# Splitting the first Q weights over two DMA queues, and normalising the first 256 columns first

## The chip, the cores and the metric

The kernel runs on one core of one Trainium2 chip. The metric is the device time of one execution in microseconds (us), the median of three runs; lower is better. TensorE (PE in the profile) multiplies matrices, VectorE (DVE) and ScalarE (ACT) work on elements, GpSimd (POOL) does small side work, and SyncE (SP) mostly issues DMA transfers. ACT can issue DMA transfers too, on a queue of its own; in the kernel before it issues none.

## The reference

Two layers, each an attention block and a feed-forward block on x of 2048 rows by 1024 columns in bf16, with the same weights in both layers:

```python
x = x + A(layernorm(x), wqkv, wo)      # 32 heads of 32; a row attends to itself and to the rows
                                       # 2, 4, ... 14 before it (8 positions, softmax)
x = x + B(layernorm(x), w1, b1, w2, b2)  # 1024 -> 3584, gelu, -> 1024
x = x + A(layernorm(x), wqkv, wo)
x = x + B(layernorm(x), w1, b1, w2, b2)
```

where `layernorm(x) = (x - mean) / sqrt(var + 1e-5)` along the 1024 columns, and `A` begins with `qkv = layernorm(x) @ wqkv`.

## The kernel before

The 2048 rows are cut into 16 tiles of 128 rows (`x[0]` to `x[15]`) and 4 groups of 512 rows. Everything the change touches lies at the very start, in the first group: x tiles 0 to 3 must be loaded, normalised and transposed (a matrix product needs the 1024 columns along the partitions, as 8 slices k = 0 to 7 of 128), and the Q weights, also 8 slices k, must be loaded. To begin early, the first pass over Q takes only tiles 0 and 1 (256 rows), two slices k at a time.

The loads, all issued by SP; one Q weight transfer carries two slices (512 KB), an x tile is 256 KB:

```python
def load_wq_piece(wt, k):
    sp.dma_start(wt[:, k % (KD // 2):k % (KD // 2) + 2, :], wqkv_v[:, k:k + 2, 0:D])

load_x(0, 0, 2)                                   # x[0], x[1]
wq_first = [wpool.tile([P, KD // 2, D], BF16, name="wt") for _ in range(2)]
for k in range(0, KD, 2):                         # k = 0,1 | x[2] | 2,3 | x[3] | 4,5 | 6,7
    load_wq_piece(wq_first[k // (KD // 2)], k)
    if k < 4:
        load_x(0, 2 + k // 2, 3 + k // 2)
```

`vec`, `act`, `pool` and `sp` are wrappers that keep the instructions of an engine in program order while `on` is set. The helper that records them is line 92, so nearly all work in the profile is on L92; matrix products are on L117, and transposes on TensorE on L211. The normalisation of the first group:

```python
def ln_first():
    vec.on = act.on = True
    def stats(tt):                # DVE: mean and variance; ACT: square root
        ... vec.bn_stats(...) x2; vec.bn_aggr(...)
        act.activation(stds[tt][:], mvs[tt][:, 1:2], ACT.Sqrt, bias=eps_t[:])
    def norm(tt, bounds=(0, D)):  # DVE: 1/std, then (x - mean) * rstd over each column range
        ...
    stats(0)
    stats(1)
    xn0 = norm(0)
    xn1 = norm(1, (0, 2 * P, D))
    transpose_on_pe(xn0, xa[0][:, 0, :, :], [(0, 2, act.copy), (2, 8, act.copy)])
    transpose_on_pe(xn1, xa[0][:, 1, :, :], [(0, 2, vec.tensor_copy)])
    transpose_on_pe(xn1, xa[0][:, 1, :, :], [(2, 8, act.copy)])
    stats(2)
    stats(3)
    for tt in range(2, 4):
        first_late.append((norm(tt), xa[0][:, tt, :, :]))
    vec.on = act.on = False
    act.hold()
```

`transpose_on_pe` writes slices of a normalised tile, transposed, into PSUM, and copies them into `xnT`. The first pass over Q, on tiles 0 and 1, with the transposes of tiles 2 and 3 put in between (`first_late`):

```python
for kq in range(4 if n == 0 else 0):      # two slices k each
    for c in range(7):                    # seven of the eight 128-column chunks of Q
        first[c] = qkv_chunk(wq, c, xnT, first.get(c), kq * (KD // 4), (kq + 1) * (KD // 4), 0, 2)
        if (kq, c) == (2, 3):
            transpose_on_pe(*first_late.pop(0), [(0, KD, act.copy)])
        if (kq, c) == (3, 4):
            ...
            transpose_on_pe(*first_late.pop(0), [(0, KD, act.copy)])
```

The launch, in order: 14 matrix products on zeros keep TensorE busy until the first data come (`warm_up(14)`), then `ln_first()`, then small constants on GpSimd (`build_constants()`), then the rest of the kernel, which the change doesn't touch.

```python
pool.on = True
warm_up(14)
ln_first()
first = build_constants()
... load_x(1); the stages of the four groups and the two layers
```

Transfers that SP or ACT issue signal their landing on one of eight semaphores, which the building layer deals out in turn over both engines. A transfer that is given a semaphore again is held back by a wait, at its issuing engine, until the transfer that had that semaphore before has landed.

Of the kernel before, what the change touches and what calls it, by code (L numbers as in the profile page):

```python
# [8 lines left out]
ACT = mybir.ActivationFunctionType  # L9
ALU = mybir.AluOpType  # L10
AX = mybir.AxisListType
BF16 = mybir.dt.bfloat16
F32 = mybir.dt.float32
# [4 lines left out]
def kernel(  # L18
# [18 lines left out]
    P = 128  # L37
# [68 lines left out]
    def dep_order(dependent, dependency, why):  # L106
        tc.add_manual_dep(dependent.ins, dependency.ins.name,
                          mybir.DependencyInfo(mybir.DependencyClass.NoSync, mybir.DependencyReason.SCHED_ONLY), reason=why)
# [12 lines left out]
    def load_x(g, t0=0, t1=NTT):  # L121
        for tt in range(t0, t1):
            t = g * NTT + tt
            sp.dma_start(x[t][:], x_in[t * P:(t + 1) * P, :])
# [6 lines left out]
            tiles.append(wt)  # L131
        return tiles

    def load_wq_piece(wt, k):
        sp.dma_start(wt[:, k % (KD // 2):k % (KD // 2) + 2, :], wqkv_v[:, k:k + 2, 0:D])

    load_x(0, 0, 2)
    wq_first = [wpool.tile([P, KD // 2, D], BF16, name="wt") for _ in range(2)]
    for k in range(0, KD, 2):
        load_wq_piece(wq_first[k // (KD // 2)], k)  # L140
        if k < 4:
            load_x(0, 2 + k // 2, 3 + k // 2)

    warm = bigp.tile([P, P], BF16, name="big")
    vec.memset(warm[:], 0.0)
    mhalf = const.tile([P, 1], F32, name="mhalf")
# [1 line left out]
    eps_t = const.tile([P, 1], F32, name="eps_t")  # L148
    pool.memset(eps_t[:], EPS)
    one = const.tile([P, 1], F32, name="one")  # L150
    act.activation(one[:], eps_t[:], ACT.Sqrt)
    ident = const.tile([P, P], BF16, name="ident")
    make_identity(nc, ident[:])
# [4 lines left out]
    mv_ahead = const.tile([P, NTT, 2], F32, name="mv_ahead")  # L158
    rstd_ahead = const.tile([P, NTT, 1], F32, name="rstd_ahead")

    def build_constants():
        pool.memset(mask[:], 0.0)
        first = smp.tile([H, W - 1, HALO], F32, name="z")
        pool.memset(first[:], 0.0)
        for w in range(W - 1):
            pool.memset(first[:, w, 0:HALO - DIL * w], -1e9)
        return first

    def load_b1(q):
        js = slice(q * (KF // 4), (q + 1) * (KF // 4))  # L170
# [37 lines left out]
    def transpose_on_pe(xn, out, parts):  # L208
        pst = psum.tile([P, KD, P], BF16, name="acc", bufs=8)
        for k in range(parts[0][0], parts[-1][1]):  # L210
            pe(nc.tensor.transpose(pst[:, k, :], xn[:, k * P:(k + 1) * P], ident[:]))  # L211
        for k0, k1, copy in parts:
            copy(out[:, k0:k1, :], pst[:, k0:k1, :])
# [5 lines left out]
        xn = ln_norm(t, mv, rstd)  # L219
        last_transpose[0] = sp.dma_start_transpose(xnT[:, tt, :, :], xn[:].rearrange("s (k p) -> s k p", p=P))  # L220

    first_late = []

    def ln_first():

        xa[0] = new_xnT()
        vec.on = act.on = True
        mvs = {}
        stds = {}

        def stats(tt):
            st6 = lnp.tile([P, 2, 6], F32, name="stats")
            for h in range(2):
                vec.bn_stats(st6[:, h, :], x[tt][:, h * HALF:(h + 1) * HALF])
            mvs[tt] = lnp.tile([P, 2], F32, name="mv")
            vec.bn_aggr(mvs[tt][:], st6[:])
            stds[tt] = lnp.tile([P, 1], F32, name="std")
            act.activation(stds[tt][:], mvs[tt][:, 1:2], ACT.Sqrt, bias=eps_t[:])

        def norm(tt, bounds=(0, D)):  # L240
            rstd = lnp.tile([P, 1], F32, name="rstd")
            vec.reciprocal(rstd[:], stds[tt][:])
            xn = lnp.tile([P, D], BF16, name="xn", bufs=3)
            for lo, hi in zip(bounds[:-1], bounds[1:]):
                vec.tensor_scalar(out=xn[:, lo:hi], in0=x[tt][:, lo:hi], scalar1=mvs[tt][:, 0:1], scalar2=rstd[:],
                                  op0=ALU.subtract, op1=ALU.mult)
            return xn

        stats(0)
        stats(1)  # L250
        xn0 = norm(0)
        xn1 = norm(1, (0, 2 * P, D))
        transpose_on_pe(xn0, xa[0][:, 0, :, :], [(0, 2, act.copy), (2, 8, act.copy)])
        transpose_on_pe(xn1, xa[0][:, 1, :, :], [(0, 2, vec.tensor_copy)])
        transpose_on_pe(xn1, xa[0][:, 1, :, :], [(2, 8, act.copy)])
        stats(2)
        stats(3)
        for tt in range(2, 4):
            first_late.append((norm(tt), xa[0][:, tt, :, :]))
        vec.on = act.on = False  # L260
        act.hold()

    def new_xnT(pool=None):
        return (pool or xnp).tile([P, NTT, KD, P], BF16, name="xnT")
# [35 lines left out]
    def gen_qkv(n, defer=False, qk_pool=None, v_late=False, qk_next=None, v_first=False, mix=0):  # L300
        g = n % NG
        xnT = xa.pop(n)
        s = st[n]
        s["prods"] = []
        qk_pool = qk_pool or attp
        if v_first:
            wv = load_qkv(2)
        wq = wq_first if n == 0 else load_qkv(0)
        if not v_first:
            wk = load_qkv(1)  # L310

        def values():
            vT = attp.tile([P, NCH, HALO + T], BF16, name="vT", bufs=2)
            s["vT"] = vT
            act.on = n > 2
            if g == 0:
                pool.memset(vT[:, :, 0:HALO], 0.0)
            else:
                (act.copy if n > 1 else pool.tensor_copy)(vT[:, :, 0:HALO], st[n - 1]["vT"][:, :, T:T + HALO])
            act.on = False  # L320
            for c in range(NCH):
                ps = qkv_chunk(wv, c, xnT)
                act.copy(vT[:, c, HALO:], ps[:])
                yield

        if v_first:
            yield from values()
            wk = load_qkv(1)
        if n == 0:
            load_x(2)  # L330
            early_tiles = ln_early((1, None), (2, qk_next))
            for _ in range(NTT):
                next(early_tiles)
            wv = load_qkv(2)
            for _ in early_tiles:
                pass
            load_x(3)
        qT = qk_pool.tile([P, NCH, T], BF16, name="qT")
        first = {}
        for kq in range(4 if n == 0 else 0):  # L340
            for c in range(7):
                first[c] = qkv_chunk(wq, c, xnT, first.get(c), kq * (KD // 4), (kq + 1) * (KD // 4), 0, 2)
                if (kq, c) == (2, 3):
                    transpose_on_pe(*first_late.pop(0), [(0, KD, act.copy)])
                if (kq, c) == (3, 4):
                    for done in range(2):
                        act.copy(qT[:, done, 0:2 * P], first[done][:, 0:2 * P])
                    transpose_on_pe(*first_late.pop(0), [(0, KD, act.copy)])
                    act.hold()
        if n == 0:  # L350
            first[7] = qkv_chunk(wq, 7, xnT, t0=0, t1=2)
        for c in list(first)[2:]:
            act.copy(qT[:, c, 0:2 * P], first[c][:, 0:2 * P])
        kT = qk_pool.tile([P, NCH, HALO + T], BF16, name="kT")
        s["qT"], s["kT"] = qT, kT
        act.on = n > 2
        if g == 0:
            pool.memset(kT[:, :, 0:HALO], 0.0)
        else:
            (act.copy if n > 1 else pool.tensor_copy)(kT[:, :, 0:HALO], st[n - 1]["kT"][:, :, T:T + HALO] if n < 3 else khalo[:])  # L360
        act.on = False

        def query(c):
            t0 = 2 if n == 0 else 0
            ps = qkv_chunk(wq, c, xnT, t0=t0)
            act.copy(qT[:, c, t0 * P:], ps[:, t0 * P:])

        def key(c):
            ps = qkv_chunk(wk, c, xnT)
            act.copy(kT[:, c, HALO:], ps[:])  # L370
            if not defer:
                new_prod(n, c)

        ahead = mix or NCH
        turns = [(query, c) for c in range(ahead)]
        for c in range(NCH):
            turns.append((key, c))
            if ahead + c < NCH:
                turns.append((query, ahead + c))
        for i, (chunk, c) in enumerate(turns):  # L380
            if i == NCH and n > 0 and not v_late and not v_first:
                wv = load_qkv(2)
            chunk(c)
            yield
        if g + 1 < NG and n > 1:
            act.copy(khalo[:], kT[:, :, T:T + HALO])
        if not v_first:
            if v_late:
                wv = load_qkv(2)
            yield from values()  # L390
# [160 lines left out]
    def warm_up(count):  # L551
        ps = acc_tile()
        for _ in range(count):
            mm(ps[:], lhsT=warm[:], rhs=warm[:].unsqueeze(1).to_broadcast([P, NTT, P]), start=True, stop=True)
# [59 lines left out]

    pool.on = True
    warm_up(14)
    ln_first()
    first = build_constants()
    with tc.tile_pool(name="early", bufs=1) as early:
        load_x(1)  # L620
        stage(gen_qkv(0, qk_next=early), sides=at(9, ln_stats_ahead, 2, NTT - 2) + at(14, pool.dma_start, mask[0::NTT, :, :], first[:]) + at(11, ln_end) + at(14, load_b2))
# [60 lines left out]
```

## Time and profile before

| | |
|---|---|
| time, median of 3 runs | 1230.46 us (1230.24 to 1230.65) |
| span of the profiled execution | 1228.4 us |
| TensorE busy | 1221.6 us, 99% |
| DVE / ACT / GpSimd busy | 861.5 / 315.6 / 120.9 us |
| first real matrix product on the weights begins at | 8.26 us |
| DMA moved | 226.64 MB, mean 185 GB/s |

The page gives each engine's busy time, then the span in 40 slices, the DMA queues, and the chain of work that ended last, followed back from the last instruction. A slice is 30.7 us long, so the whole start that the change touches lies inside the first one; it is read from the timeline (start, duration, engine, line, operation, `out<-in`, count, and in brackets how long the engine had been idle and what released it) and from a table of busy times, granted clock and DMA rate in stretches of half a microsecond. The duration of a merged entry runs from the start of its first instruction to the end of its last. A DMA issue has two times: how long the issuing engine needed to issue it, and how long after that start its data had landed.

### The profile page before, as it was taken

The page shows a single profiled execution, that of the slowest core. Times are in us where ns is not written, and L with a number is a line of the kernel's source. Part 1 is how long each engine was busy: PE and PEld are TensorE (multiplying, and loading weights), DVE is VectorE, ACT ScalarE, POOL GpSimd, SP SyncE. Part 2 cuts the span into 40 slices and gives each one's busy share as a digit, 9 for nine tenths or more (in the row PEclk, how much of TensorE's full clock was granted, in tenths as well). Part 3 has the DMA queues.
Part 4 walks back from the last instruction along what each step waited for, and adds up shares of the span by engine and source line. Part 5 has one row for each costly group of instructions (what it writes and reads, how often), then busy time and mean ns, then how long its engine had stood idle before and what let it go on. Part 6 is the DMA issues. An engine that isn't in the chain of part 4 may idle for free.

```text
span 1228.4 us, 13955 instructions
## 1 busy us (share of the span) xinstructions
PE 1221.6 (99%) x5720; PEld 632.7 (52%) x5770; DVE 861.5 (70%) x912; ACT 315.6 (26%) x497; POOL 120.9 (10%) x219
## 2 busy tenths in 40 slices
PE   9999999999999999999999999999999999999998
PEld 7666544456444564446544465444654444444444
DVE  7999896998898999375993759937599797011001
ACT  5343253014310233202431024410244001300310
POOL 2330025010101101100001000000000002000000
PEclk9999999999999999999999999999999999999999
DMA  9965674766638645856557565576664558446441
GB/s 302 290 206 164 176 233 151 202 178 199 219 128 245 188 150 166 239 170 175 161 158 230 172 171 181 157 216 201 171 200 147 186 194 209 149 159 194 156 135 52
DMA packets 223647, 226.64 MB, mean 185 GB/s; under 512 B 71824, under 2 KB 190752, under 8 KB 221536
## 3 DMA queue, kind: packets, MB, share of 16 engines
q1 hardware_dynamic: 214704, 208.69, 56.3%
q0 software_dynamic: 8880, 17.07, 4.2%
q8 instruction: 45, 0.74, 0.2%
q14 instruction: 18, 0.15, 0.0%
HBM read 189.01 MB, written 4.19 MB: 157 GB/s over the span
## 4 chain that ended last, share of the span: by engine, by line
PE 99%; DVE 0%; issue 0%; DMA 0%
PE acc L117 99%; DMA x<-in_A_x_dram 0%; DVE stats L92 0%; PE acc L211 0%; DVE xn L92 0%; DVE x L92 0%; DVE mv L92 0%; DVE rstd L92 0%
## 5 line engine op out<-in xcount | busy, mean ns | idle before, releaser
L117 PE MATMUL acc<-xnT,wt 128*128 128x512 bf16 (+1 forms) x3392 | 720.3, 375 | 0.1
L117 PEld LDWEIGHTS <-wt 128*128 128x128 bf16 x3392 | 400.8, 120 | 317.4
L117 PE MATMUL acc<-wt,hT 128*128 128x512 bf16 (+1 forms) x1780 | 386.0, 376 | 2.1
L117 PEld LDWEIGHTS <-hT 128*128 128x128 bf16 x1820 | 178.1, 98 | 209.0
L92 DVE TENSOR_TENSOR big<-big 128x1024 bf16<-128x1024 bf16 (+2 forms) x184 | 244.8, 1359 | 2.2
L92 ACT ACTIVATE hT<-acc,b1T 128x512 bf16<-128x512 f32 x224 | 152.1, 687 | 325.9 <-PE acc L117 325.8
L92 DVE TENSOR_TENSOR big<-qT,kT 128x4096 bf16<-128x4096 bf16 x64 | 143.8, 2283 | 36.3 <-ACT kT L92 35.9
L92 DVE TENSOR_TENSOR big<-abc,vT 128x4096 bf16<-128x4096 bf16 x64 | 144.6, 2284 | 11.0 <-DMA abc<-a 7.1
L92 DVE TENSOR_TENSOR tmp<-acc,b2bc 128x512 f32<-128x512 f32 x56 | 38.6, 689 | 159.8 <-PE acc L117 156.7
L92 ACT CAST qT<-acc 128x512 bf16<-128x512 f32 (+1 forms) x72 | 38.0, 543 | 276.8 <-PE acc L117 274.6
L117 PE MATMUL acc<-wt,oT 128*128 128x512 bf16 x440 | 97.6, 379 | 0.4
L92 DVE BATCH_NORM_STATS2 stats<-x 128x6 f32<-128x512 bf16 x116 | 77.4, 681 | 6.0 <-DMA x<-in_A_x_dram 5.0
L117 PEld LDWEIGHTS <-oT 128*128 128x128 bf16 x448 | 43.8, 98 | 53.0 <-issue 0.3
L92 DVE TENSOR_TENSOR x<-acc,big 128x512 bf16<-128x512 f32 (+1 forms) x9 | 5.7, 632 | 90.0 <-PE acc L117 90.0
L92 POOL TENSOR_TENSOR rstd<-mv,eps_t 128x1 f32<-128x1 f32 x54 | 16.7, 308 | 524.2 <-DVE mv L92 524.2
L92 ACT CAST vT<-acc 128x512 bf16<-128x512 f32 x64 | 37.4, 585 | 101.9 <-PE acc L117 101.9
L92 ACT CAST kT<-acc 128x512 bf16<-128x512 f32 x64 | 37.3, 584 | 64.5 <-PE acc L117 64.5
L92 DVE TENSOR_TENSOR x<-acc,x 128x512 bf16<-128x512 f32 x64 | 42.9, 670 | 5.1 <-PE acc L117 4.7
L92 DVE TENSOR_SCALAR xn<-x,mv,rstd 128x1024 bf16<-128x1024 bf16 (+2 forms) x53 | 28.5, 540 | 20.1 <-POOL rstd L92 19.9
L92 DVE TENSOR_TENSOR x<-tmp,x 128x512 bf16<-128x512 f32 x56 | 38.6, 689 | 1.4
L92 POOL DMA_DIRECT2D big<-big x24 | 13.3, 563 | 212.5 <-DVE big L92 212.5
L92 ACT ACT_TABLE_LOAD x17 | 21.8, 1283 | 38.9 <-DVE e L92 30.5
(62 smaller groups left out, 285.4 us busy)
## 6 DMA issues: line engine op xcount, KB each, us to landing
wt<-in_B_w_dram SPq DMA_DIRECT2D x56, 1024.0 KB, 5.6
wt<-in_B_w_dram SPq DMA_DIRECT2D x64, 896.0 KB, 4.8
wt<-in_A_wqkv_dram SPq DMA_DIRECT2D x46, 1024.0 KB, 5.6
wt<-in_A_wo_dram SPq DMA_DIRECT2D x16, 1024.0 KB, 5.0
abc<-a POOLq DMA_DIRECT2D x32, 256.0 KB, 4.6
big<-big POOLq DMA_DIRECT2D x24, 256.0 KB, 3.8
x<-in_A_x_dram SPq DMA_DIRECT2D x16, 256.0 KB, 7.1
out_dram<-x SPq DMA_DIRECT2D x31, 128.0 KB, 1.8
```

Source lines behind the costliest of these rows:

```text
L92: inst = f(*args, **kwargs)
L117: return pe(nc.tensor.matmul(*args, **kwargs))
```

## The change

The change means to let the first real matrix products start earlier, with less of x and less of the weights. It has these parts:

- The first x tile comes in two transfers of 512 columns, so that its statistics can begin with the first half.
- Each Q weight slice is a transfer of its own (256 KB). The even ones and the last are issued by SP, slices 1, 3 and 5 by ACT, which waits for GpSimd's last small fill first ("behind the first x tiles").
- Columns 0 to 255 of both tiles are normalised first. Before the first matrix product on weights stand 10 transposes (slices 0, 1 of both tiles, then 2 to 7 of tile 0) in place of 16; the other six of tile 1 stand behind the fourth chunk of the first pass.
- The small constants are built ahead of `ln_first()`.

```diff
-    def load_wq_piece(wt, k):
-        sp.dma_start(wt[:, k % (KD // 2):k % (KD // 2) + 2, :], wqkv_v[:, k:k + 2, 0:D])
-
-    load_x(0, 0, 2)
+    def load_wq_piece(k, engine):
+        return engine.dma_start(wq_first[k // (KD // 2)][:, k % (KD // 2), :], wqkv_v[:, k, 0:D])
+
+    for h in range(2):
+        sp.dma_start(x[0][:, h * HALF:(h + 1) * HALF], x_in[0:P, h * HALF:(h + 1) * HALF])
+    load_x(0, 1, 2)
     wq_first = [wpool.tile([P, KD // 2, D], BF16, name="wt") for _ in range(2)]
     for k in range(0, KD, 2):
-        load_wq_piece(wq_first[k // (KD // 2)], k)
+        load_wq_piece(k, sp)
         if k < 4:
             load_x(0, 2 + k // 2, 3 + k // 2)
 
+    load_wq_piece(KD - 1, sp)
...
+    act.on = True
     act.activation(one[:], eps_t[:], ACT.Sqrt)
...
+            filled[w] = pool.memset(first[:, w, 0:HALO - DIL * w], -1e9)
...
+    def load_wq_on_act():
+        act.on = True
+        for k in range(1, KD - 2, 2):
+            load = load_wq_piece(k, act)
+            if k == 1:
+                (the first of them waits for filled[W - 2], the last small fill on GpSimd)
+        act.on = False
...
         stats(0)
         stats(1)
-        xn0 = norm(0)
-        xn1 = norm(1, (0, 2 * P, D))
-        transpose_on_pe(xn0, xa[0][:, 0, :, :], [(0, 2, act.copy), (2, 8, act.copy)])
-        transpose_on_pe(xn1, xa[0][:, 1, :, :], [(0, 2, vec.tensor_copy)])
-        transpose_on_pe(xn1, xa[0][:, 1, :, :], [(2, 8, act.copy)])
-        stats(2)
-        stats(3)
+        for tt in range(2):
+            norm(tt, 0, 2 * P)
+        norm(0, 2 * P, D)
+        transpose_on_pe(xns[0], xa[0][:, 0, :, :], [(0, 2, act.copy)])
+        transpose_on_pe(xns[1], xa[0][:, 1, :, :], [(0, 2, vec.tensor_copy)])
+        norm(1, 2 * P, D)
+        transpose_on_pe(xns[0], xa[0][:, 0, :, :], [(2, KD, act.copy)])
+        act.on = False
+        act.hold()
+        first_late.append((xns[1], xa[0][:, 1, :, :], [(2, KD, act.copy)]))
         for tt in range(2, 4):
-            first_late.append((norm(tt), xa[0][:, tt, :, :]))
-        vec.on = act.on = False
-        act.hold()
+            stats(tt)
+            norm(tt)
+            first_late.append((xns[tt], xa[0][:, tt, :, :], [(0, KD, act.copy)]))
+        vec.on = False
...
-                if (kq, c) == (2, 3):
-                    transpose_on_pe(*first_late.pop(0), [(0, KD, act.copy)])
+                if (kq, c) in ((0, 3), (2, 3)):
+                    transpose_on_pe(*first_late.pop(0))
+                    (at kq == 0 also: the square roots of tiles 2 and 3 stand behind tile 1's copy on ACT)
...
     warm_up(14)
+    first = build_constants()
+    load_wq_on_act()
     ln_first()
-    first = build_constants()
```

In the built program the changed ACT begins in this order: square root of a constant; the three weight transfers, slices 1, 3, 5; the two square roots for tiles 0 and 1; the copies of transposes. The transfers of slices 1, 3 and 5 carry the same semaphores as those of slices 0, 2 and 4, which SP issues, and so each waits at ACT for the landing of its neighbour. Further on, SP issues the first half of the V weights ahead of the DMA transposes of the next group, and the second half between the last two of them; before, both stood behind the first four.

## The prediction

> **What bounds the kernel now.** I read the page first, its chain of work that ended last and then its busy times:
>
> ```profile
> PE 99%; DVE 0%; issue 0%; DMA 0%
> PE 1221.6 (99%) x5720; PEld 632.7 (52%) x5770; DVE 861.5 (70%) x912; ACT 315.6 (26%) x497; POOL 120.9 (10%) x219
> ```
>
> TensorE is the bound, and it has no holes to fill: 1228.4 - 1221.6 = 6.8 us in the whole span. But "busy" includes the 14 products on zeros. The product on weights that counts begins at 8.26 us, and 1228.4 - 8.26 = 1220.1 us follow. So the change can gain only by moving that start, at most a few us of 1230, and it loses whatever it delays the start by or puts into the stream behind it. What sets the start is in the timeline of the first 9 us:
>
> ```profile
> 0.74 0.87 SPq L92 DMA_DIRECT2D x<-in_A_x_dram  x2
> 0.99 6.02 PE L117 MATMUL acc<-big 128*128 128x512 bf16 x14 [0.99 <-DVE big L92]
> ...
> 3.46 1.29 DVE L92 BATCH_NORM_STATS2 stats<-x 128x6 f32<-128x512 bf16 x2 [2.52 <-DMA x<-in_A_x_dram]
> ...
> 5.02 0.29 ACT L92 ACTIVATE std<-mv,eps_t 128x1 f32<-128x1 f32 x1 [2.78 <-DVE mv L92]
> ...
> 6.17 0.21 DVE L92 BATCH_NORM_AGGREGATE mv<-stats 128x2 f32<-128x12 f32 x1
> 6.30 0.11 DVE L92 RECIPROCAL rstd<-std 128x1 f32<-128x1 f32 x1
> ...
> 6.44 0.55 DVE L92 TENSOR_SCALAR xn<-x,mv,rstd 128x1024 bf16<-128x1024 bf16 x1
> ...
> 7.05 1.35 PE L211 MATMUL acc<-ident,xn 128*128 128x128 bf16 x16
> 7.10 0.73 DVE L92 TENSOR_SCALAR xn<-x,mv,rstd 128x256 bf16<-128x256 bf16 x2
> ...
> 7.82 0.29 DVE L92 COPY xnT<-acc 128x256 bf16<-128x256 bf16 x1
> ...
> 8.26 4.15 PE L117 MATMUL acc<-xnT,wt 128*128 128x256 bf16 x36
> ```
>
> The reader should see a chain on DVE: x[0] at 3.46, statistics of two tiles until 6.38, two normalisations, the copy ending at 8.11, the product at 8.26. ACT gives a small but necessary link: without the square root at 5.02 there is no reciprocal and no normalisation.
>
> The transfers are read from issue time plus time to landing. x[0] 0.74 + 2.7 = 3.4; x[1] 1.2 + 3.1 = 4.3; slices 0,1 1.66 + 5.6 = 7.3; x[2] 2.13 + 5.8 = 7.9; slices 2,3 2.64 + 6.6 = 9.2; x[3] 3.11 + 6.8 = 9.9; slices 4,5 3.62 + 7.6 = 11.2 us. SP issues the first seven by 4.1 us, but they land one after the other until 11.2: from 2 us on the engines are saturated and a transfer's place in the line decides. The rate, by half microseconds (the last column):
>
> ```profile
> 4.00:4.50 0.50, 0.50 (x3) 0.23 (x2) 0.50 (x2) 0.00 (x0) 0.00 (x0) 1.00 1.11 238
> 6.50:7.00 0.50, 0.50 (x2) 0.00 (x0) 0.50 (x2) 0.21 (x1) 0.00 (x0) 1.00 1.09 410
> ```
>
> **The Trainium skill, three places.** "Perfetto Trace Analysis", DMA Instruction — HWDGE: the issuing sequencer itself sits in the semaphore wait of a transfer, and is free for its next instruction only once the transfer is issued. The trace agrees for SP: the load behind the group's x tiles starts issuing at 9.24 us, just when slices 2,3 land, and everything behind it waits too. No ACT transfer exists in it. "DMA: Bandwidth & Descriptors", Issuing engines are not separate DMA queues: transfers of all issuers share the same 16 engines, and a second issuer saves only issue time. The trace agrees that issue is not the bound (0.4 us an issue against 0.7 us per 256 KB at 390 GB/s). "TensorE: Matmul & The Clock Gate", Part 1: an idle window of about 3.4 us halves the TensorE clock, a busy one restores it. The zero products start (6.51 - 0.99) / 13 = 0.425 us apart; 128x512 products later go 49 in 10.74 us, 0.219 each, though the granted clock column says 1.00 for both.
>
> **The change part by part.**
>
> *Intended gains.* Ten transposes instead of 16 ahead of the first product, and 256 instead of 1024 columns of tile 0 normalised ahead of tile 1. DVE's last statistics could end about 0.3 us earlier with the halves of x[0]; against that, x[1] is issued one issue (0.4 us) later, and 768 columns of tile 0 (0.47 us) now stand on DVE between the second normalisation and the copy. I put the first product at about 8.0 to 8.1, a gain of 0.2 us, if ACT were free.
>
> *ACT is not free.* In the built program ACT's three transfers stand ahead of its square roots. Slice 1 waits for slice 0 to land, slice 3 for slice 2, slice 5 for slice 4. So the square root of tile 0, ready to run at about 4.7, must wait until slice 4 has landed. Nothing computes with slice 4 for another pass; only the shared semaphore ties them.
>
> *When slice 4 lands.* On SP it is the eighth issue, with x[0] to x[3] and slices 0, 2, 4: 7 x 262,144 bytes = 1.835 MB. In the kernel before, the same 1.835 MB were complete with slices 2,3, at 9.24 us. Slice 0 ends at 0.786 MB, between x[1] (4.3) and slices 0,1 (7.3): about 5.9 us. Then ACT issues slice 1, whose bytes flow from about 7 beside SP's. Ahead of slice 4 this puts up to 0.262 MB / 390 GB/s = 0.67 us: slice 4 lands at 9.2 to 9.9, I take 9.8.
>
> *From there to the first product.* Issue of slice 5 0.43: 10.25. Square roots of both tiles, 0.29 each: the first ends at 10.55. Reciprocal 0.11, normalisation of 256 columns 0.35, the same for tile 1 (0.5), 768 columns 0.47, copy 0.29, with gaps of 0.05: copy ends at about 12.2, the first product at 12.35. That is 12.35 - 8.26 = **+4.1 us**.
>
> *Behind it.* Six transposes move into the stream: 8 took 0.45 us in the chain, so +0.34 us. Tile 1's columns 256 to 1023 are transposed after the fourth chunk (8 x 0.11 = 0.88 after the start) and copied by ACT in 0.81 us; the remaining six products of the pass take 0.66 us, so the second pass waits some **0.3 us** for the copy. Tiles 2 and 3 are ready about 2 and 1 us ahead of need. Slice 5, issued at 9.8, lands near 13.6 and is wanted near 16.
>
> *Clock.* The zero products end at 7.05, and TensorE then stands from there to the first transposes near 11.1, 4 us. That is close to the window: if it drops, the first 3 to 6 us of products run at half rate, 1.5 to 3 us lost. I give it 1 in 3, so about +0.7 on average.
>
> *Later.* The second half of the V weights stands behind the fifth DMA transpose; I expect it by about 41 to 42 us, when it is wanted near 42. On average +0.2.
>
> Sum: 4.1 + 0.34 + 0.3 + 0.7 + 0.2 = 5.6; without the clock 4.9. I predict 1230.46 + 5.1 = **1235.6 us**.
>
> **Rivals.**
> 1. *The intended effect.* ACT's waits pass early, or its square roots overtake them, and the first product comes at 8.0 with fewer transposes in front: 1230.0 to 1230.4. For it: the profile shows ACT idle from 2.2 to 5.0 us, and slice transfers half as large land sooner. Against it: the order on ACT, and slice 4's place behind 1.57 MB of a saturated line. I give it 8%.
> 2. *Slice 4 comes early.* If the line runs near 400 GB/s from the start, in place of 238 at 4.0 to 4.5 us, slice 4 lands near 7.5 and the loss is 2 us: 1232.5. Against it: the first three microseconds are slow with one queue already. I give it 12%.
> 3. *The clock falls too.* Four us of idle TensorE plus half rate: 1237 to 1239. A third of what is left.
> 4. *The V weights come late.* If each DMA transpose again takes 3.6 us to issue, as the first did at 16.68, their second half lands 2 to 3 us after need: 1237 to 1238. For it: the new order on SP, and little to spare before: the second half landed at 27.1 + 8.8 = 35.9, and the V products began near 37.2 (the first copy of V at 38.93, less 8 x 0.219). Against it: the later transposes of that row were issued in 1.3 us each.
>
> **Range and chances.** Main line 1234.5 to 1236, clock and V weights above, rivals 1 and 2 below: 1232.2 to 1238.5 holds 8 in 10. 2% is 24.6 us, three times the whole start before the first product, so within 2% is nearly certain.
>
> **What would show each step.** In the changed timeline: ACT's three issues, the last near 9.8; the square roots right behind, near 10.3, with a DMA as what released them; DVE idle from about 6 to 10.5; a hole on PE from 7 to 11; first product at 12.3. Products of 256 columns 0.11 us apart show a warm clock, 0.21 a cold one. A first product before 9 us would refute the central step; a first product at 12.3 with an unchanged end would mean that time is given back later, which I hold impossible with TensorE at 99%.

## The result and the profile after

| | before | changed |
|---|---|---|
| time, median of 6 runs | 1230.24 us (1229.99 to 1230.65) | 1236.26 us (1236.05 to 1237.3) |
| ratio | | 1.005, 95% interval 1.0037 to 1.0063 |
| span of the profiled execution | 1228.4 us | 1234.5 us |
| first product on weights | 8.26 us | 11.97 us |

The change costs 6.0 us. The timeline of the changed kernel (start, duration, engine, line, operation, and in brackets the idle time before it and what ended it; ACTq is ACT's sequencer issuing transfers) answers to the lines shown of before:

```profile
4.63 0.21 DVE L92 BATCH_NORM_AGGREGATE mv<-stats 128x2 f32<-128x12 f32 x1
...
6.03 3.52 ACTq L92 DMA_DIRECT2D wt<-in_A_wqkv_dram  x3
...
9.59 0.48 ACT L92 ACTIVATE std<-mv,eps_t 128x1 f32<-128x1 f32 x2 [7.36 <-DMA wt<-in_A_wqkv_dram]
9.92 0.16 DVE L92 RECIPROCAL rstd<-std 128x1 f32<-128x1 f32 x1 [3.46 <-ACT std L92]
...
10.52 1.66 PE L227 MATMUL acc<-ident,xn 128*128 128x128 bf16 x10 [3.91 <-DVE xn L92]
...
11.97 2.03 PE L117 MATMUL acc<-xnT,wt 128*128 128x256 bf16 x8
...
12.28 1.25 PEld L117 LDWEIGHTS <-wt 128*128 128x128 bf16 x7 [0.24 <-DMA wt<-in_A_wqkv_dram]
```

Variance and mean of tile 0 are ready at 4.84 us, as wished a little earlier than before. The square root that needs them runs at 9.59. Between stand ACT's three transfers: the first is issued at 6.03, the last at 9.21, and the bracket names a DMA, not DVE, as what ended ACT's idle 7.36 us. DVE then waited 3.46 us for the root, TensorE 3.91 us for DVE. The chain that ended last, up to 15 us (start, duration, what), goes the same way:

```profile
4.03 5.16 DMA wt<-in_A_wqkv_dram
...
9.21 0.34 ACTq L92
...
9.59 0.30 ACT std L92
...
10.97 1.21 PE acc L227 x8
```

Read it from the top: the transfer of slice 4, issued by SP at 4.03, lands 5.16 us later at 9.19; 0.02 us after that ACT issues slice 5; then come the root, the normalisation, the transposes and the products. No arithmetic in this chain uses slice 4. The two transfers before it went the same way: slice 0 (issued at 2.13) landed after 3.8 us, at 5.93, and ACT issued slice 1 at 6.03; slice 2 (3.08) landed after 4.3 us, at 7.38, and slice 3 was issued at 7.4.

The second loss is in the TensorE table by microseconds (stretch, its length, TensorE busy with count, granted clock, DMA share, GB/s):

```profile
8.00:9.00 1.00, 0.00 (x0) 1.00 0.99 344
9.00:10.00 1.00, 0.00 (x0) 0.67 1.06 406
10.00:11.00 1.00, 0.42 (x3) 0.50 1.05 401
...
16.00:17.00 1.00, 1.00 (x10) 0.92 1.05 389
```

TensorE ran dry at 6.60 us, and in the tenth microsecond its clock fell to half (at 9.34 by finer stretches); it came back at 16.17, more than five microseconds after work had resumed at 10.52.

Where the two kernels do the same again, the bookkeeping closes. The products behind the transposes of tile 3, in the kernel before and in the changed kernel:

```profile
14.89 45.37 PE L117 MATMUL acc<-xnT,wt 128*128 128x256 bf16 x247
20.99 3.23 PE L117 MATMUL acc<-xnT,wt 128*128 128x256 bf16 x28
```

They start 6.10 us later, which is the difference of the spans (1234.5 - 1228.4 = 6.1). To within 0.1 us nothing is lost or won behind that point. Of the 6.10, 11.97 - 8.26 = 3.71 lie ahead of the first product; 2.39 lie behind it.

### The profile page after: what moved, and what is told of

Read it like the earlier page. It is cut to its first block, busy times and chain, and to the rows that moved or that the text cites. A ratio compares the mean times of both kernels' runs of the same rounds, so it can differ in the third digit from the quotient of the medians.

```text
span 1234.5 us, 13960 instructions
## 1 busy us (share of the span) xinstructions
PE 1223.7 (99%) x5720; PEld 634.1 (51%) x5770; DVE 862.8 (70%) x913; ACT 316.0 (26%) x497; POOL 124.1 (10%) x219
## 4 chain that ended last, share of the span: by engine, by line
PE 99%; DMA 0%; issue 0%; SPq 0%; DVE 0%; ACTq 0%; ACT 0%
PE acc L117 98%; DMA wt<-in_A_wqkv_dram 0%; SPq L92 0%; PE acc L227 0%; DVE xn L92 0%; DVE x L92 0%; ACTq L92 0%; ACT std L92 0%; DVE rstd L92 0%
## 5 line engine op out<-in xcount | busy, mean ns | idle before, releaser
L92 POOL DMA_DIRECT2D abc<-a x32 | 17.7, 559 | 135.5 <-DVE a L92 135.5
```

The lines of the kernel that those rows point to most:

```text
L92: inst = f(*args, **kwargs)
```

## The experiments

Theory A: ACT is held at its transfers by semaphores that they share with slices 0, 2 and 4, and all that stands behind them on ACT is held too; then the clock falls. Theory B: two queues on the same DMA engines delay each other's data. Theory C: the column order itself costs. Below, "marker" is the start of the products behind tile 3's transposes, 14.89 us before and 20.99 in the changed kernel, from each run's timeline; "first product" is that on weights. The kernel before ran beside each group, at 1230.24 us for the changed kernel and at 1230.37 to 1230.68 for the others. First product and marker are those of the one execution that was profiled; medians are over 5 to 13 executions.

| run | median us (range) | ratio to before, 95% interval | first product | marker |
|---|---|---|---|---|
| changed kernel | 1236.26 (1236.05 to 1237.3) | 1.005 (1.0037 to 1.0063) | 11.97 | 20.99 |
| two queues only | 1234.71 (1234.23 to 1234.76) | 1.0035 (1.0022 to 1.0048) | 11.54 | 19.36 |
| columns only | 1230.95 (1230.68 to 1231.57) | 1.0003 (0.9995 to 1.0012) | 8.22 | 15.55 |
| all slices on SP | 1231.35 (1230.67 to 1232.17) | 1.0007 (0.9999 to 1.0015) | 8.38 | 15.71 |
| x[0] halves only | 1230.19 (1230.03 to 1231.58) | 0.9998 (0.999 to 1.0007) | 8.62 | 15.65 |
| GpSimd as second queue | 1231.51 (1231.04 to 1233.61) | 1.0008 (1.0 to 1.0017) | 8.46 | 15.80 |
| no wait for the fill | 1233.84 (1232.18 to 1235.25) | 1.0028 (1.0017 to 1.004) | 9.90 | 18.42 |
| 32 zero products | 1234.61 (1234.52 to 1235.02) | 1.0035 (1.0021 to 1.0049) | 11.83 | 19.55 |
| roots first | 1237.41 (1236.78 to 1238.33) | 1.0057 (1.0044 to 1.0071) | 10.41 | 21.95 |
| slice 1 on SP | 1234.76 (1233.81 to 1236.03) | 1.0035 (1.0021 to 1.0048) | 10.79 | 19.84 |

### Two queues only

The kernel before with single slices, 1, 3 and 5 on ACT, and the constants ahead; x[0], columns and transposes as before.

```diff
-        load_wq_piece(wq_first[k // (KD // 2)], k)
+        load_wq_piece(k, sp)            # k = 0, 2, 4, 6, and 7 behind them
...
+    first = build_constants()
+    load_wq_on_act()                    # k = 1, 3, 5
     ln_first()
-    first = build_constants()
```

> The kernel before with one part of the change: single slices, 1, 3 and 5 on ACT behind the fill, constants ahead. x[0] in one piece, the old order of columns and transposes. Theory A: ACT's three transfers share semaphores with slices 0, 2 and 4 again, the square root waits until slice 4 lands near 9 us, first product near 12 us, clock falls, total 1235.5 to 1237. Theory B: the same. Theory C: no loss, near 1230.2.

Its timeline:

```profile
5.24 3.66 ACTq L92 DMA_DIRECT2D wt<-in_A_wqkv_dram  x3
...
8.95 0.48 ACT L92 ACTIVATE std<-mv,eps_t 128x1 f32<-128x1 f32 x2 [6.71 <-DMA wt<-in_A_wqkv_dram]
...
11.54 5.33 PE L117 MATMUL acc<-xnT,wt 128*128 128x256 bf16 x36
```

The hold is there without any of the column order: roots behind the last transfer, first product at 11.54. This part alone makes 4.47 of the 6.10 us at the marker. It came 0.8 us below the lower edge expected: slice 4 landed earlier, its roots running at 8.95, and the clock, which fell here too, was down from 10.65 to 14.06 us only. Theory C can't be the main cause.

### Columns only, all slices on SP, halves only

Three runs without a transfer on ACT. Columns only has the loads of before under the new order of columns and transposes; against the changed kernel:

```diff
-    for h in range(2):
-        sp.dma_start(x[0][:, h * HALF:(h + 1) * HALF], ...)
-    load_x(0, 1, 2)
+    load_x(0, 0, 2)
+        (two slices a transfer, all on SP)
-    load_wq_on_act()
```

> The kernel before with the other part of the change: first 256 columns of both tiles first, 10 transposes ahead of the first product and six behind, constants ahead; loads as before (two slices a transfer, x[0] in one piece, all on SP). Theory A: no hold, first product 8.0 to 8.3, total 1229.9 to 1230.6, no measurable loss. Theory C: slower than before by 1 us or more.

```profile
8.22 1.07 PE L117 MATMUL acc<-xnT,wt 128*128 128x256 bf16 x8
...
9.12 0.50 PE L224 MATMUL acc<-ident,xn 128*128 128x128 bf16 x6
...
9.46 0.82 PE L117 MATMUL acc<-xnT,wt 128*128 128x256 bf16 x6
...
10.51 2.56 PE L117 MATMUL acc<-xnT,wt 128*128 128x256 bf16 x22 [0.23 <-ACT xnT L92]
```

The first product comes at 8.22, not earlier than before in any way that matters: DVE still has 768 columns of tile 0 to normalise ahead of the copy. Then the six transposes are paid behind it: from 9.12 to the next product at 9.46, 0.34 us. The six products from 9.46 stand 0.11 us apart, so the seventh was due near 10.12; it starts at 10.51, 0.39 us late, and waits for ACT's copy of tile 1 (the bracket shows only 0.23 us of it, as it counts from a modelled end). The marker is 0.66 us late. The timing, +0.5 us with an interval that holds 1, doesn't contradict this and can't prove it. Transposes moved behind the first product are not removed from TensorE.

The two parts together make 4.47 + 0.66 = 5.13 of the 6.10 us. For the rest the clock is enough, by an estimate: in the changed kernel it came back 2.11 us later than with two queues only (16.17 against 14.06), and at half rate about half of that, 1.06 us, is lost.

All slices on SP keeps the whole change but the second queue:

```diff
         load_wq_piece(k, sp)
+        load_wq_piece(k + 1, sp)
...
-    load_wq_piece(KD - 1, sp)
...
-    load_wq_on_act()
     ln_first()
```

> All eight Q weight slices on SP, in order of k; everything else of the change stays. Theory A (ACT is held at its transfers by shared semaphores until slice 4 has landed, and so are the square roots behind them; then the clock falls): no transfer stands on ACT, the square root runs near 4.7 us, the first product on weights comes at 7.9 to 8.2 us, no hole, total 1229.7 to 1230.6 us. Theory B (two queues share one set of DMA engines and delay the x tiles and slices): also fast, as one queue is left. Theory C (the column order itself costs, six transposes among the first Q chunks and the DVE copy behind 768 more columns): the loss stays, 1233 us or more.

```profile
4.64 0.29 ACT L92 ACTIVATE std<-mv,eps_t 128x1 f32<-128x1 f32 x1 [2.40 <-DVE mv L92]
```

The root ran at 4.64 us, released by DVE, and the first product came at 8.38: with the second queue taken away, 5.3 of the 6.1 us at the marker go. The time was 0.75 us above the expected range's upper edge: I had counted on the column order to gain, and in the profile it costs (marker 0.82 us late; in the timing +0.98 us, with an interval that just holds 1). Statistics of x[1] began only at 5.12, after 0.52 us of waiting for data, against 4.90 before.

Halves only asks whether that is the price of loading x[0] in two transfers; against the kernel before:

```diff
-    load_x(0, 0, 2)
+    for h in range(2):
+        sp.dma_start(x[0][:, h * HALF:(h + 1) * HALF], x_in[0:P, h * HALF:(h + 1) * HALF])
+    load_x(0, 1, 2)
```

> The kernel before with x[0] in two column halves, nothing else. The all-on-SP run came 0.4 us above the run with the column order alone; that had the halves and the single slices in addition, and its x[1] was waited for until 5.12 us. If the halves are what costs: statistics of x[0] start near 3.1 in place of 3.46, those of x[1] near 5.1 in place of 4.90, first product near 8.45, total 1230.5 to 1230.8. If the single slices are: first product 8.0 to 8.2, total 1230.0 to 1230.3.

In its profile tile 0's statistics start at 3.04, tile 1's at 5.21 after 0.64 us of waiting, and the first product comes at 8.62: the gain at the first half is lost at x[1]. But the timed runs show no difference from before (ratio 0.9998), and the profiled execution took 1230.67 us, 0.48 above this kernel's median. One profile can't settle an effect of this size, and what the halves cost stays open.

### GpSimd as the second queue, and no wait for the fill

These separate "two queues" from "a hold at the second". GpSimd's transfers carry semaphores of a kind of their own:

```diff
-            load = load_wq_piece(k, act)
+            load = load_wq_piece(k, pool)
-            if k == 1:
-                (wait for the last small fill)
```

> The changed kernel with slices 1, 3 and 5 issued by GpSimd behind its fills (from about 1.9 us) in place of ACT. GpSimd's transfers use other semaphores, so nothing waits; two queues stay. Theory A: square root near 4.7 us, first product 8.0 to 8.6, total 1229.8 to 1231. Theory B: the sharing stays, first product beyond 10 us, total above 1233.

```profile
1.81 1.80 POOL L92 DMA_DIRECT2D wt<-in_A_wqkv_dram  x3
...
4.74 0.29 ACT L92 ACTIVATE std<-mv,eps_t 128x1 f32<-128x1 f32 x1 [2.51 <-DVE mv L92]
...
8.46 1.07 PE L117 MATMUL acc<-xnT,wt 128*128 128x256 bf16 x8
```

GpSimd issues all three from 1.81 us on, nothing holds ACT, the root runs at 4.74 and the first product comes at 8.46. Two queues sharing the DMA engines cost next to nothing here beyond the column order (marker 15.80 against 15.71 with one queue, medians 1231.51 and 1231.35). As the main cause of the changed kernel's time, theory B falls. The run does not test a second queue that runs ahead: from 1.7 to 4 us all 367 packets are of SP's queue, and GpSimd's data move only after that.

The other run keeps ACT as issuer and removes the wait for the fill; in the built program the three transfers then stand early enough in the dealing out to get fresh semaphores:

```diff
             load = load_wq_piece(k, act)
-            if k == 1:
-                (wait for the last small fill)
```

> The changed kernel, only without the wait of ACT's first transfer for the last small fill on GpSimd. In the built program ACT's three transfers are then dealt out among the first eight, each with a fresh semaphore, so none waits; the later ones of SP wait instead. Two queues, slices and column order stay. Theory A: ACT issues its three by 3.6 us, square root near 4.7, first product near 8.0 to 8.5 (the slices of ACT now compete with x[1] and slice 0, some 0.3 us), total 1229.8 to 1231. Theory B: two queues still share, the first product stays beyond 10 us, total 1233 to 1236. Theory C: stays above 1233.

```profile
0.91 1.35 ACTq L92 DMA_DIRECT2D wt<-in_A_wqkv_dram  x3
...
6.62 1.29 DVE L92 BATCH_NORM_STATS2 stats<-x 128x6 f32<-128x512 bf16 x2 [1.04 <-DMA x<-in_A_x_dram]
```

A miss: expected up to 1231, measured 1233.84. The hold is gone, but ACT issues from 0.91 us, before SP has issued x[1] (1.66), and the weights take bandwidth from x: between 1 and 3 us ACT's queue moved 0.14 of the 0.27 MB. x[1] lands 4.9 us after its issue, at 6.6, in place of 3.2 us in the changed kernel; tile 1's statistics wait for it, the first product comes at 9.90, and the clock falls at 9.77 and returns at 13.18. That fall is not in every execution: in two of the six the granted clock was 1.000 on average, and they took 1232.18 and 1232.34 us; the four with a fall took 1233.78 to 1235.25. So theory B is true in a weaker form: a second queue harms when it runs ahead of the data that the chain needs first. The wait for the fill had its purpose; its price is that the transfers then stand late enough in the order to be given used semaphores.

### 32 zero products

```diff
-    warm_up(14)
+    warm_up(32)
```

> The changed kernel with 32 products on zeros in place of 14. At full clock 18 more take 18 x 0.216 = 3.9 us, from 6.6 to 10.5 us, just the hole. Theory A with the clock as its second part: first product still near 12.0 us minus the 0.3 to 0.5 us that cold transposes cost, products 0.11 us apart from the start, total 2.0 us below the changed kernel, 1234.2. If the clock column were only a record and the products after 12 us were slow because slices came late, it stays at 1236.2.

The changed kernel with the hole filled:

```profile
9.68 0.48 ACT L92 ACTIVATE std<-mv,eps_t 128x1 f32<-128x1 f32 x2 [7.45 <-DMA wt<-in_A_wqkv_dram]
...
11.83 0.30 PE L117 MATMUL acc<-xnT,wt 128*128 128x256 bf16 x1
...
12.29 0.99 PE L117 MATMUL acc<-xnT,wt 128*128 128x256 bf16 x7 [0.15 <-DMA wt<-in_A_wqkv_dram]
...
13.44 0.83 PE L117 MATMUL acc<-xnT,wt 128*128 128x256 bf16 x6
...
14.49 2.56 PE L117 MATMUL acc<-xnT,wt 128*128 128x256 bf16 x22 [0.23 <-ACT xnT L92]
```

Root and first product are where they were (9.68 and 11.83), but now products follow 0.11 us apart and the clock column says 1.00 throughout. The time is 1.65 us lower, and the ranges don't touch. I had expected 2.0. The rest is visible: at full clock TensorE reaches two other waits that the slow clock had hidden. By the starts of the products, 0.11 us apart, the one behind slice 1 comes 0.35 us late (12.29, due at 11.94), and the one behind ACT's copy of tile 1 0.39 us late (14.49, due near 14.10).

### Roots first

```diff
         stats(0)
         stats(1)
+        load_wq_on_act()                # square roots stand ahead, copies behind
         for tt in range(2):
             norm(tt, 0, 2 * P)
...
-    load_wq_on_act()
     ln_first()
```

> The changed kernel with one move: on ACT the square roots of tiles 0 and 1 stand ahead of the three transfers, which keep their shared semaphores and still wait for slices 0, 2 and 4. Theory A, sharpened (whatever stands behind the transfers on ACT waits, not the square roots as such): square root near 4.7 and 6.4 us, DVE normalises by 7.6, TensorE does its first transposes near 7.0, but ACT's copy of tile 0's first slices now waits until about 9.6, so the first product comes near 10.1 us, between the 8.4 without transfers on ACT and the 11.97 of the change; total 1232.8 to 1234, the upper end if the clock falls. If only the square root's own wait mattered, first product near 8.4 and 1231.4.

```profile
4.61 0.29 ACT L92 ACTIVATE std<-mv,eps_t 128x1 f32<-128x1 f32 x1 [2.37 <-DVE mv L92]
...
7.47 2.48 ACTq L92 DMA_DIRECT2D wt<-in_A_wqkv_dram  x3
...
9.99 1.07 ACT L92 COPY xnT<-acc 128x256 bf16<-128x256 bf16 x2 [2.29 <-DMA wt<-in_A_wqkv_dram]
10.41 0.36 PE L117 MATMUL acc<-xnT,wt 128*128 128x256 bf16 x1 [1.18 <-ACT xnT L92]
...
13.09 1.71 PE L117 MATMUL acc<-xnT,wt 128*128 128x256 bf16 x7 [2.33 <-DMA wt<-in_A_wqkv_dram]
```

The hold moved as expected: roots at 4.61 and 7.41 (the second 1.0 us later than expected, as x[1] was waited for until 5.84), and ACT's first copy waits until 9.99 behind the transfers, giving a first product at 10.41. The total was missed by 3.4 us. TensorE did one product and then waited 2.33 us for a DMA: slice 1. It was issued at 7.47, behind both roots, and landed 5.6 us later, at 13.09; the clock was at half from 10.47 to 17.29. In the changed kernel slice 1 was issued at 6.03 and took 6.2 us, landing at 12.23, just beside the first product. Theory A was incomplete: the shared semaphore holds not only what stands behind the transfers on ACT but also slice 1 itself, and freeing the roots alone exposes that.

The records by queue show where the 6.2 us go. In the changed kernel, no packet of ACT's queue (q10) stands in the stretches from 6 to 9 us; SP's queue (q1) has them all. First the stretch from 8 to 9 us, where q1 is alone, then q10 in the stretch from 9 to 10 us (packets, MB, share of 16 engines):

```profile
q1 hardware_dynamic: 190, 0.34, 98.9%
...
q10 hardware_dynamic: 36, 0.07, 18.9%
```

What SP had issued before was served first. Why the engines didn't take turns earlier was not tried and stays open.

### Slice 1 on SP

```diff
         load_wq_piece(k, sp)
+        if k == 0:
+            load_wq_piece(1, sp)
...
-        for k in range(1, KD - 2, 2):
+        for k in range(3, KD - 2, 2):       # the first of them waits for the fill
```

> The changed kernel with slice 1 on SP right behind slice 0; ACT keeps only slices 3 and 5. In the built program the semaphores shift with it: slice 3 now waits for slice 0, slice 5 for x[2] (fifth 256 KB of the line after x[0], x[1] and slices 0 and 1), not for slice 4. Theory A (ACT's square roots run when the last transfer that stands before them has been issued): held until x[2] lands, 1.31 MB down the line, near 7.5 us in place of 9.2; square root near 7.9, first product 2.4 us later, near 10.3; the second product does not wait, as slice 1 lands by 7 us. Total 1232.6 to 1233.4 at full clock, up to 1235 if the clock falls. If the late slice 1 (12.2 us) were the true bound and the square roots only ran beside it: first product as early, but total near 1231.3, or, if something else holds TensorE until 12 us, still 1236.

```profile
5.61 2.75 ACTq L92 DMA_DIRECT2D wt<-in_A_wqkv_dram  x2
...
8.40 0.48 ACT L92 ACTIVATE std<-mv,eps_t 128x1 f32<-128x1 f32 x2 [6.17 <-DMA x<-in_A_x_dram]
...
10.79 1.91 PE L117 MATMUL acc<-xnT,wt 128*128 128x256 bf16 x8
```

With one transfer more ahead of them the semaphores shift, and ACT waits for x[2] in place of slice 4. The bracket names an x tile; x[2], issued at 3.07, landed after 4.9 us, near 8.0, where ACT issued its second transfer, and the root moves from 9.59 to 8.40 (7.9 was expected, with x[2] landing near 7.5). The first product follows 2.39 us behind it, as it does in the changed kernel (11.97 - 9.59 = 2.38). No product waits for slice 1. The clock fell here too (at 8.35 us, back at 15.18), which puts the time at the upper end expected. With slice 1 early and a shorter hold, clock and column order included, the kernel still costs 4.1 us (1234.76 against 1230.68 beside it).

## Why the prediction was right

Predicted were 1235.6 us, within 1232.2 to 1238.5; 1236.26 was measured. Its central step, the square roots held until slice 4 has landed, is shown: by the chain, by its removal (all on SP, GpSimd), and by moving what ACT waits for (slice 1 on SP). That the tie is a shared semaphore is read from the built program; the traces show the waits and the landings that end them. That the total came within 0.7 us is in part luck, as errors in its terms cancel:

| term | predicted us | measured us | how |
|---|---|---|---|
| first product later | 4.1 | 3.71 | 11.97 - 8.26 |
| six transposes behind it | 0.34 | about 0.34 | with columns only, 9.12 to 9.46; the half rate is in the next line |
| clock at half rate | 0.7 on average | about 2.1 | products at half rate from 11.97 to 16.17: half of 4.20 |
| wait for tile 1's copy | 0.3 | 0 | hidden by the slow clock; 0.39 with 32 zero products |
| V weights late | 0.2 | 0 | no shift behind the marker |
| sum | 5.6, of which I took 5.1 | about 6.15, against 6.10 at the marker | |

- **Slice 4's landing** was mis-sized by 0.6 us: predicted 9.8, measured 9.19. I had put up to 0.67 us of slice 1's bytes ahead of it. None ran ahead of it, and the plain analogy, the same 1.835 MB complete at 9.24 before, was nearly exact. From the start of the root to the first product I had 12.35 - 10.25 = 2.10 us; measured were 2.38, and 2.15 at full clock (32 zero products), so most of the difference is the clock. My sum was loose there too: the parts that I list behind 10.55 make 1.72 us, so the copy ends at 12.27 before any gap, not at 12.2.
- **Slice 1** was missing from the sum. The hidden second consequence of the same wait, its landing at 12.23, falls almost on the first product, so it cost little here; it would have ruled had the roots been freed.
- **The clock** was named with 1 in 3. It fell in all six executions (granted 0.997 to 0.999 on average), and is the largest term that the average under-sized. I asked only how long TensorE stands idle; where the idle time lies in what looks like a rhythm of the clock seems to matter as well (last section). The start came 0.4 us earlier than predicted, the clock took 1.4 more, and the 0.3 and 0.2 us for the copy and the V weights were not paid. The total is therefore closer than its parts.
- **The intended effect** would have been no gain even without the hold: 0.2 us expected at the first product, 0.04 measured with columns only, and the transposes come back behind it. The columns-only term, +0.66 us at the marker, contains them; its timing can't be told from before.
- **The Trainium skill.** "Perfetto Trace Analysis", DMA Instruction — HWDGE, says that the issuing sequencer holds the wait; the changed trace agrees for ACT, idle 7.36 us with a DMA as what ended it. "DMA: Bandwidth & Descriptors", Issuing engines are not separate DMA queues, agrees in substance: GpSimd as a second issuer gained nothing over SP alone. "TensorE: Matmul & The Clock Gate", Part 1, gives a window of about 3.4 us, idle for the fall and busy for the return, that runs free of the kernel. The traces agree: the clock fell 2.7 us into a hole of 3.9 us, and also after 1.8 us of full idleness with thin work behind it (no wait for the fill), so no idle stretch of 3.4 us is needed; but it stays low for 3.41 us or twice that (last section).

No version here beats both kernels. Before, TensorE stands idle for only about 0.3 us between the zero products and the first product (7.05 to 8.26, less 16 transposes of 0.056 each), so in that execution the order of columns had no more than that to win as long as the 14 zero products stay.

## What to carry to other kernels

Before a transfer is put on a compute engine's queue, look at what it waits for in the built program, including the wait for a reused semaphore, and at what stands behind it on that engine: everything there, needed or not, waits for the same thing. Ask the same of the transfer itself, as its own data come late too. Work moved from ahead of the first product to behind it still takes its time on TensorE, and a hole of a few microseconds can cost half as much again in clock (3.9 us and about 2.1 here).

## What the runs showed of the hardware that I had not expected

- A transfer newly issued on ACT's idle queue at 6.03 us moved its first packet only after 9 us and landed 6.2 us after issue, while SP's backlog was served.
- The clock fell at different distances from the last zero product, and in every trace with a fall near the start it stayed at half for 3.41 us or for twice that:

| run | last zero product ends | clock falls | returns | at half for | TensorE busy in the 3.41 us before the fall |
|---|---|---|---|---|---|
| changed kernel | 6.60 | 9.34 | 16.17 | 6.83 | 0.68 |
| slice 1 on SP | 6.12 | 8.35 | 15.18 | 6.83 | 1.18 |
| no wait for the fill | 6.82 | 9.77 | 13.18 | 3.41 | 1.31 |
| two queues only | 5.57 | 10.65 | 14.06 | 3.41 | 0.57 |
| roots first | 5.47 | 10.47 | 17.29 | 6.82 | 1.14 |

- These figures fit a clock that is set anew every 3.41 us, by how busy TensorE was in the stretch just ended. In the last two runs the stretch before the one in the table had TensorE busy for 1.74 and 1.84 us of 3.41 (3.83 to 7.24 and 3.64 to 7.05), and brought no fall; those in the table, up to 1.31 us, did. The return took more: the stretch behind the fall with 2.17 us busy (changed kernel) or 2.37 us (slice 1 on SP) left the clock at half, and stretches with 3.34 us or more brought it back. Where the stretches begin differs from execution to execution, which would also explain why the kernel without the wait for the fill has executions with a fall and without. That this is how the clock is set was not tested by a run of its own. With 1.2 to 1.3 us of idleness (GpSimd, all on SP) it did not fall at all.
- The clock column stands at 1.00 during the first zero products too, which start 0.425 us apart, against 0.219 us for products of the same shape later: the column doesn't show that first slow stretch.
- ACT issued transfers from 0.91 us on while its table load (0.74 to 2.02 us) was still running (no wait for the fill).
